# Attention with a gated MLP on one core: opening memsets on two engines, last residual rows in the q/k buffers, another order table

## Chip, core and metric

One core of a Trainium2 chip. The metric is device time in microseconds (us) for one execution of the whole program, taken as the median of three runs. For every kernel there is also one profiled execution, which has a time of its own and a span (first to last instruction) inside it.

## What is computed

Four batches, twelve heads, 448 positions, 64 numbers per head; all in 32-bit floats.

```
scores = (q @ k.T) / sqrt(64), causal mask, softmax with 1e-9 added to the sum
x      = attention output, heads side by side                    # 4 x 448 x 768
h      = gelu_tanh(x @ w_in)                                     # 768 -> 1024
u, v   = halves of h;   v = layernorm(v) * g_ln
v_s    = w_sg @ v + b_sg                                         # mixes positions, 448 x 448
out    = x + (u * v_s) @ w_out                                   # 512 -> 768
```

## The kernel before

The work is cut into 24 pairs of heads (six per batch) and one MLP per batch. A pair (`pair`, L602) loads q and k (L609), makes scores on TensorE in two operations S0 and S1 (L618), adds the mask and takes the row maximum on VectorE (L632, eight operations), takes exponentials with row sums on ScalarE (L640, ten operations, each an ACTIVATE and an accumulator read), turns the weights by TensorE transposes (pairs 0 to 7, L687, evicted to the tile B at L694 or L692) or by a VectorE transpose and block moves by DMA (pairs 8 to 23, L675 and L679), multiplies with v (L718; v is loaded at L712) and scales by the inverse row sums, which take a way through DRAM (L659, L662). The result goes to DRAM as the residual x (L754) and, split into two parts, into the MLP. The MLP (`mlp`) has per batch four groups for v (v0 to v3), four for u, four for the mixing (s) and six for the output (o0 to o5), all as chunks of up to three matmuls at L779. The groups o0 to o5 read back two residual tiles at a time (`res`, L898), add (L910) and store (L914 in the last batch, L918 in the others).

The weight w_in comes in as twelve tiles of 512 KB (W1 to W12, loaded at L552 into three `vn` buffers). Each is prepared by ScalarE (L554), VectorE (L556, L558) and GpSimd (L561, L562). Four tiles of w_sg (SG, L536 to L541) and sixteen of w_out are prepared in a like manner.

Every step is an "op" that is registered with `Order.add`. `Order.plan` sorts the ops of each engine (and of SyncE, which issues all DMAs, in order, each waiting for its semaphores at the head of the queue) by a greedy plan with modelled durations: `dur` of a DMA's issue, `size` for its transfer, and `COLD` = (6.0, 1.35), a factor on transfers issued before 6.0 us. The priorities in that plan are the places in the table `ORDER`, which is written out by hand. Each engine's order in the planned program of the kernel before is the table's own, engine by engine.

What comes first: `consts` (L491, GpSimd: identity and masks), `consts2` (L505, VectorE: zeros into the pad columns of all six P tiles, three fillings of the three `sm` tiles, `mhalf`, the pad rows of `wsg`), `warm` (L521, VectorE: zeros for seven matmuls at L528 that read no data and only keep TensorE busy). VectorE's queue is `consts2`, `warm`, then the masks of pair 0 (two small ones, L556 of W1, a large one).

Score tiles come from six PSUM banks, two for each S op. The fourth S op in the order waits for the exponentials that read the first one's banks, and so on. The tags `qk` (three buffers) and `res` (two buffers) have tiles of the same shape, 128 x 2 x 448.

```
od.add("pool", 2.5, consts, w=["ident", "mask"], at=-9)
od.add("dve", 1.6, consts2, w=["P", "sm", ("wsg", "pad")], at=-9)
od.add("act", 0.2, lambda: nc.scalar.activation(out=pad[:, 0:1], in_=mhalf, func=AF.Exp), ["sm"], ["table"], -30)
od.add("dve", 0.45, warm, w=[wz], at=-30)
rr = buf(two, "res", [128, 2, S])
```

Of the kernel before, what the change touches and what calls it, by code (L numbers as in the profile page):

```python
# [973 lines left out]
```

## Time and profile before

| | before |
|---|---|
| median of 3 runs | 358.58 us (358.38 to 360.68) |
| profiled execution, its own time | 359.28 us |
| its span | 357.5 us, 6919 instructions |
| busy: TensorE / VectorE / ScalarE / GpSimd | 343.3 / 258.7 / 204.2 / 148.9 us |
| chain that ended last | TensorE 55%, ScalarE 15%, issue 11%, VectorE 8%, DMA 5% |

PE is TensorE, PEld its weight loads, DVE VectorE, ACT ScalarE, POOL GpSimd, SP the queue that issues the DMAs. Busy time is time with an instruction in flight; a TensorE operation that stands between two of its own matmuls may count as busy or not. A view of windows gives busy time per engine in a stretch; the chain follows the last instruction back, each time to what released it; a timeline row has the start, the duration and, in brackets, the idle time before it and what ended it. The clock column is the granted TensorE clock as a share of 2.4 GHz.

### The profile page before, as it was taken

To read this page: it belongs to the slowest core of one execution; us is meant where nothing else is said; L and a number is where in the kernel's file an instruction comes from. 1 tells how busy PE (TensorE), PEld (TensorE's weight loads), DVE (VectorE), ACT (ScalarE), POOL (GpSimd) and SP (SyncE) were. 2 spreads that over 40 slices of the span, in tenths; PEclk is the share of its full clock that TensorE was granted. 3 is DMA by queue.
4 is the path that set the end of the run, shared out by engine and by line. 5 is a ranking of instruction groups with operands and counts; after the bars stand their busy time and mean duration, and the time that the engine had idled before them with its cause. 6 is when DMAs were issued, how large, how long until landed. Compare 5 with 4: busy or idle time off the path is not lost.

```text
span 357.5 us, 6919 instructions
## 1 busy us (share of the span) xinstructions
PE 343.3 (96%) x2231; PEld 269.9 (75%) x2231; DVE 258.7 (72%) x801; ACT 204.2 (57%) x658; POOL 148.9 (42%) x185
## 2 busy tenths in 40 slices
PE   5799899999999999999999999999999999999995
PEld 1455566768788887677888887877997797889994
DVE  2877979789999887979889477469679541475512
ACT  2789997975887665682857551544545600344400
POOL 2244777865698820303204821101526510342640
PEclk9969999999999999999999999999999999999999
DMA  7848768989864768987819757985641656700014
GB/s 260 296 126 297 252 202 284 334 283 254 274 173 143 202 157 237 263 272 248 275 22 269 230 149 231 242 284 148 221 119 38 179 146 198 255 5 1 0 53 154
DMA packets 37973, 69.50 MB, mean 194 GB/s; under 512 B 3889, under 2 KB 18993, under 8 KB 37937
## 3 DMA queue, kind: packets, MB, share of 16 engines
q1 hardware_dynamic: 37936, 69.06, 63.5%
q8 instruction: 18, 0.29, 0.3%
q14 instruction: 19, 0.15, 0.1%
HBM read 39.68 MB, written 12.58 MB: 146 GB/s over the span
## 4 chain that ended last, share of the span: by engine, by line
PE 55%; ACT 15%; issue 11%; DVE 8%; DMA 5%; POOL 3%; SPq 2%; DVEq 0%; ACTq 0%; POOLq 0%
PE m L779 41%; ACT P L640 11%; PE s L618 6%; PE o L718 5%; DMA B<-P 5%; DVE P L675 2%; DVE s L632 2%; SPq L679 2%; ACT B L694 2%; PE tx L687 1%; PE ty L687 1%; POOL tmp L884 1%; POOL x L760 1%; PE m L528 1%; ACT vn L554 1%
## 5 line engine op out<-in xcount | busy, mean ns | idle before, releaser
L640 ACT ACTIVATE P<-s,ngm 128x448 f32<-128x448 f32 (+3 forms) x240 | 101.0, 426 | 40.1 <-DVE ngm L632 26.5
L632 DVE CUSTOM_DVE_ANT_0 s<-s,mask 128x192 f32<-128x192 f32 (+3 forms) x192 | 75.2, 444 | 14.6 <-PE s L618 10.5
L779 PE MATMUL m<-win,x 128*128 128x512 f32 (+1 forms) x264 | 66.3, 397 | 0.3 <-ACT P L640 0.3
L779 PE MATMUL m<-x,win 128*128 128x448 f32 x288 | 63.6, 370 | 0.3
L779 PE MATMUL m<-g,wout 128*128 128x448 f32 x288 | 63.1, 369 | 0.4 <-ACT P L640 0.4
L618 PE MATMUL s<-qk 64*66 64x64 f32 (+3 forms) x384 | 55.7, 412 | 2.7 <-ACT P L640 2.3
L779 PEld LDWEIGHTS m<-g,wout 128*128 128x128 f32 x288 | 53.2, 188 | 6.7 <-ACT P L640 1.5
L779 PEld LDWEIGHTS m<-x,win 128*128 128x128 f32 x288 | 53.2, 188 | 6.7 <-ACT P L640 1.1
L779 PEld LDWEIGHTS m<-win,x 128*128 128x128 f32 (+1 forms) x264 | 47.1, 183 | 12.2 <-ACT P L640 0.7
L618 PEld LDWEIGHTS s<-qk 64*128 64x128 f32 (+1 forms) x384 | 33.5, 182 | 25.4 <-issue 13.9
L718 PE MATMUL o<-B,vraw 128*64 128x64 f32 (+4 forms) x672 | 47.8, 293 | 1.3 <-ACT P L640 0.6
L675 DVE STREAM_TRANSPOSE P<-P 128x1024 f32<-128x1024 f32 x32 | 39.2, 1230 | 12.6 <-DMA B<-P 9.3
L640 ACT ACTIVATION_READ_ACCUMULATOR P<-s,ngm 128x1 f32 (+1 forms) x240 | 46.9, 195 | 0.0
L718 PEld LDWEIGHTS o<-B,vraw 128*64 128x64 f32 x672 | 32.8, 137 | 16.0 <-issue 6.6
L779 PE MATMUL m<-wsg,vn 128*128 128x448 f32 x176 | 39.0, 369 | 0.0
L760 POOL TENSOR_TENSOR x<-xt,x 128x448 fp32r<-128x448 f32 x24 | 28.8, 1205 | 22.3 <-ACT x L759 12.6
L779 PEld LDWEIGHTS m<-wsg,vn 128*128 128x128 f32 x176 | 32.7, 188 | 3.2 <-DVE g L792 0.2
L833 POOL TENSOR_TENSOR mv<-mv,mhalf 128x1 f32<-128x1 f32 (+1 forms) x16 | 9.2, 578 | 58.7 <-DVE mv L831 58.6
L884 POOL TENSOR_TENSOR tmp<-tmp,g 128x448 f32<-128x448 f32 x16 | 18.3, 1150 | 20.1 <-DVE tmp L880 20.0
L787 ACT ACTIVATE tmp<-m 128x448 f32<-128x448 f32 (+1 forms) x28 | 15.4, 565 | 18.9 <-PE m L779 17.4
L759 ACT ACTIVATE x<-xt 128x448 fp32r<-128x448 f32 x18 | 10.2, 574 | 27.9 <-DVE xt L748 27.8
L632 DVE DVE_READ_ACCUMULATOR2_ANT ngm<- 128x1 f32 (+1 forms) x192 | 25.7, 134 | 0.0
(72 smaller groups left out, 382.7 us busy)
## 6 DMA issues: line engine op xcount, KB each, us to landing
B<-P SPq DMA_DIRECT2D x64, 256.0 KB
qk<-in_qk_dram SPq DMA_DIRECT2D x24, 448.0 KB
vn<-in_w_in_dram SPq DMA_DIRECT2D x12, 512.0 KB
vraw<-in_vP_dram SPq DMA_DIRECT2D x24, 256.0 KB
rb<-rd SPq DMA_DIRECT2D x24, 256.0 KB
xd<-xt SPq DMA_DIRECT2D x24, 224.0 KB
res<-xd SPq DMA_DIRECT2D x12, 448.0 KB
out_dram<-res SPq DMA_DIRECT2D x9, 448.0 KB
```

The lines of the kernel that those rows point to most:

```text
L618: nc.tensor.matmul(out=s[z][bk].t[0:w, col:col + n], lhsT=qk_.t[r, 0, q0:q0 + w], rhs=qk_.t[r, 1, 0:n], start=True, stop=True)
L632: nc.vector.tensor_tensor_reduce(out=o, in0=o, in1=mk, scale=-0.125, scalar=3e38, op0=ALU.add, op1=ALU.min, accum_out=ngm[ib[z]][c][0:m])
L640: act(n, lambda c=c, m=m, r0=r0, k0=k0, n=n, bk=bk, col=col, off=off, kc=kc, i=i, z=z: nc.scalar.activation(out=P[i][r0:m, off:off + n], i ...
L675: dve(PW, lambda z=z: nc.vector.transpose(A[ia][:, :, :, z, :].rearrange("p g t k -> p t g k"), P[ib[z]]), Pk[z] + ["P"], Ak, Tt, 1.105)
L679: dma(lambda i=i: nc.sync.dma_start(out=B_.t[:, 512 * i:512 * i + 512], in_=PP[ia][32 * i:32 * i + 32].rearrange("p (g n) -> p g n", g=4)) ...
L718: nc.tensor.matmul(out=dst(o.t[r]), lhsT=vr.t[:, c, r], rhs=src(z), start=first and n == 0, stop=last and n == len(lst) - 1)
L759: act(S, lambda: nc.scalar.activation(out=y.t[:, 0:S], in_=x.t, func=AF.Copy), [x], [y], Ty, True)
L760: pool_tt(S, lambda: nc.gpsimd.tensor_tensor(out=y.t[:, S + 64:], in0=x.t, in1=f(y.t)[:, 0:S], op=ALU.subtract), [x, y], [(y, 1)], Ty)
L779: nc.tensor.matmul(out=ps.t[0:l().shape[1], 0:n], lhsT=l(), rhs=rr(), start=(k == 0), stop=(k == len(mms) - 1))
L787: act(n, lambda: nc.scalar.activation(out=z(), in_=h(), func=AF.Square), [ps], [t], at)
L833: od.add("pool", 0.46, lambda mv=mv, m=m: nc.gpsimd.tensor_tensor(out=mv.t[0:m, 1:2], in0=mv.t[0:m, 1:2], in1=mhalf[0:m], op=ALU.pow), ["s ...
L884: pool_tt(S, lambda z=z, u=u: nc.gpsimd.tensor_tensor(out=z(), in0=z(), in1=u.t, op=ALU.mult), [u], [t], at)
```

## The change

1. The opening memsets are split. `consts2` on VectorE keeps the pads of P tiles 0 and 1, the filling of `sm` tile 0, and `mhalf`. A new op `consts3` on GpSimd, behind `consts`, does P tiles 2 to 5, `sm` tiles 1 and 2 and the pad rows of `wsg`. What reads P tiles 0 and 1 or `sm` tile 0 first waits for VectorE's op, the rest for GpSimd's.
2. In the last batch the residual tiles `res` are taken from the three `qk` buffers.
3. Modelled prices are set anew: `COLD` 6.0, 0.85; issue times 0.43 to 1.7 for five kinds of DMA; the size of the load of `g_ln` and `b_sg` is halved. They act only through the plan.
4. The table `ORDER` is a new one, of 1927 ops (the new op is number 2). `WHEN`, `ctx`, `seq` and `key` are bookkeeping; with `WHEN = 0, 0` the ops are registered in the old order. `xt` keeps its two buffers.

```
-SLOTS = {'qk': 3, 'B': 2, 'rb': 3, 'vraw': 2}
+SLOTS = {'qk': 3, 'B': 2, 'rb': 3, 'vraw': 2, 'xt': 2}
+WHEN = 0, 0
-COLD = 6.0, 1.35
+COLD = 6.0, 0.85
...
+    def pads(eng, ps, sms):
+        for i in ps:
+            for c in (320, 960):
+                eng.memset(P[i][:, c:c + 64], 0.0)
+        for t in sms:
+            eng.memset(t, 0.0)
+            eng.memset(t[:, :, :, 2:3], 1e-9)
+            eng.memset(t[64:128, :, 0, 0:1], 1.0)
+
     def consts2():
...
+        pads(nc.vector, (0, 1), sm[:1])
         nc.vector.memset(mhalf, -0.5)
-        nc.vector.memset(f(wsg)[64:128, 3, 1, :], 0.0)
...
+    def consts3():
+        pads(nc.gpsimd, range(2, NP), sm[1:])
+        nc.gpsimd.memset(f(wsg)[64:128, 3, 1, :], 0.0)
+
+    od.add("dve", 0.75, consts2, w=["P0", "sm0"], at=-9)
+    od.add("pool", 2.4, consts3, w=["P", "sm", ("wsg", "pad")], at=-8)
...
-        dma(load, [], [t], at - 6, n * 512, early)
+        dma(load, [], [t], at - 6, n * 512, early, dur=0.43 * len(src))
...
+        kp, ks = "P" if p % (NP // 2) else "P0", "sm" if p % NS else "sm0"
...
-                rr = buf(two, "res", [128, 2, S])
+                rr = buf(*((two, "res") if b < B - 1 else (some[SLOTS["qk"]], "qk")), [128, 2, S])
```

What the two tables say of the first ops, engine by engine (S0, S1 scores; Tx, Ty transposes; ex3, ex0, ex2, ex1, ex1b exponentials by chunk; z0 and z1 the heads of a pair; ev an eviction; V the load of v):

```
SyncE   before  qk0 W1 V0 qk1 qk2 W2 W3 gb V1 qk3 W4 qk4 ...
SyncE   after   qk0 W1 qk1 qk2 W2 W3 gb V0 V1 qk3 W4 qk4 W5 SG1 SG2 SG3 ...
VectorE before  consts2 warm, masks of pair 0: 0z1 0z0, W1/L556, 3z0 1z0 1z1 2z0, W1/L558, 2z1 3z1, masks of pair 1
VectorE after   consts2 warm, W1/L556 W1/L558, masks of pair 0: 0z0 0z1 3z0 3z1 1z0 1z1 2z0 2z1, W2/L556, masks of pair 1
ScalarE before  W1, pair 0: ex3z0 ex0z0 ex2z0 ex1z0 ex1bz0 ex1z1 ex2z1 ex3z1 ex1bz1 ex0z1, pair 1: ex3z0 ...
ScalarE after   W1, pair 0: ex3z0 ex3z1 ex0z0 ex0z1, W2, ex2z0 ex1z1, W3, ex1bz0 ex2z1, p1 ex3z1, ex1z0, p1 ex0z1 ex3z0, ex1bz1, p1 ...
TensorE before  p0S0 p0S1 p1S0 p1S1 p0Tx p0Ty p2S0 p0Tx ... p4Tx behind 1 chunk of the first MLP, p5Ty behind 2
TensorE after   p0S0 p0S1 p1S0 p1S1 p0Ty p2S0 p0Tx p0Ty ... p3Tx behind 3 chunks of the first MLP, p4Tx behind 4, p5Ty behind 6
GpSimd  after   consts consts3 W1/L561 W1/L562 W2 ...
```

In the last batch, SyncE's table now has the residual load of o0 and o1 in front of the block moves of pair 22, the one of o2 and o3 between the moves of pairs 22 and 23, and the one of o4 and o5 ahead of the first store; before, the first two stood behind all moves and the third behind two stores. TensorE's last chunks before: o3 o3 o4 o5 o5 o5 o5 o4 o3 o2 o2 o3 o4 o4; after: o1 o2 o2 o3 o5 o5 o5 o5 o4 o4 o4.

## Rows read from the trace of the kernel before

**Rows 1.** Busy time by windows; columns: stretch, length, busy (instructions), clock, DMA share, GB/s

```profile
0.00:4.00 4.00, 0.00 (x0) 0.00 (x0) 2.40 (x24) 1.49 (x2) 2.63 (x11) 1.00 0.53 167
4.00:7.20 3.20, 3.08 (x7) 0.88 (x7) 0.07 (x1) 0.66 (x1) 0.00 (x0) 1.00 0.95 289
7.20:10.00 2.80, 2.80 (x13) 1.68 (x14) 0.50 (x5) 0.00 (x0) 0.00 (x0) 1.00 1.03 417
...
16.00:24.00 8.00, 7.50 (x29) 4.49 (x29) 4.70 (x20) 7.15 (x25) 2.31 (x2) 0.57 0.40 138
24.00:30.00 6.00, 5.87 (x47) 3.37 (x47) 4.99 (x22) 5.57 (x23) 1.96 (x2) 1.00 0.86 249
30.00:54.00 24.00, 22.16 (x164) 13.76 (x163) 19.95 (x69) 23.46 (x79) 17.25 (x18) 1.00 0.77 254
54.00:120.00 66.00, 65.77 (x455) 50.27 (x454) 61.32 (x199) 50.27 (x159) 50.22 (x71) 1.00 0.78 243
```

**Rows 2.** The chain that ended last, in order of time, 0 to 60 us

```profile
0.82 0.93 DVE P L508 x12
3.00 0.43 DVE wsg L514
3.58 0.50 DVE tmp L523
4.12 3.17 PE m L528 x7
7.29 2.06 PE s L618 x8
...
9.97 0.28 DVE vn L556
...
10.95 0.73 ACT P L640 x2
...
54.49 0.66 PE ty L687 x4
55.25 1.39 PE m L779 x6
```

**Rows 3.** Timeline of the first 16 us, all engines

```profile
0.73 0.21 POOL masks.py:197 MEMSET ident<- 128x128 f32 x1 [0.29 <-POOLq L963]
...
1.25 0.47 POOL L493 MEMSET mask<- 128x448 bf16 x1
...
2.97 0.45 POOL L500 TENSOR_SCALAR_AFFINE_SELECT mask<-mask 64x320 bf16<-64x320 bf16 x1
...
6.48 0.66 ACT L554 ACTIVATE vn<-vn 128x512 f32<-128x512 f32 x1 [3.40 <-DMA vn<-in_w_in_dram]
...
9.50 0.23 DVE L632 CUSTOM_DVE_ANT_0 s<-s,mask 64x64 f32<-64x64 f32 x1 [5.44 <-PE s L618]
...
11.79 0.68 DVE L558 SCALAR_TENSOR_TENSOR vn<-vn 128x512 int32<-128x512 int32 x1
...
12.60 0.64 POOL L561 CAST win<-vn 128x512 fp32r<-128x512 f32 x1 [9.18 <-DMA vraw<-in_vP_dram]
```

**Rows 4.** Timeline of ScalarE, 18 to 26 us

```profile
20.57 0.60 ACT L694 ACTIVATE B<-tx 128x512 f32<-128x512 f32 x1 [0.56 <-PE tx L687]
...
24.28 0.60 ACT L694 ACTIVATE B<-tx 128x512 f32<-128x512 f32 x1 [0.53 <-PE tx L687]
```

**Rows 5.** Timelines of the end, in small windows

```profile
338.93 14.76 PE L779 MATMUL m<-g,wout 128*128 128x448 f32 x72
...
348.74 0.38 SPq L898 DMA_DIRECT2D res<-xd  x1
...
353.72 0.62 DVE L910 TENSOR_TENSOR res<-m,res 128x448 f32<-128x448 f32 x1
354.05 0.93 SPq L914 DMA_DIRECT2D out_dram<-res  x2
```

**Rows 6.** The chain again, 157 to 164 us: a block move

```profile
157.91 5.63 DMA B<-P
```

More of the change, by code (lines that the diff above doesn't have):

```diff
@@ L223, in __init__ @@
         self.shared, self.room, self.early = shared, room, early
-        self.bufs = {}
+        self.bufs, self.ctx, self.seq = {}, (), {}
     def add(self, eng, dur, fn, r=(), w=(), at=0.0, done=0.0, rows=1.0, size=0.0, early=0.0, shape=None, port=False,
@@ L228, in add @@
         n = len(self.ops)
+        self.seq[self.ctx] = k = self.seq.get(self.ctx, -1) + 1
+        key = self.ctx + (k,)
         deps = set()
@@ L503, in attention_gated_mlp @@
     od.add("pool", 2.5, consts, w=["ident", "mask"], at=-9)
-    def consts2():
-        for i in range(NP):
-            for c in (320, 960):
-                nc.vector.memset(P[i][:, c:c + 64], 0.0)
-        for t in sm:
-            nc.vector.memset(t, 0.0)
-            nc.vector.memset(t[:, :, :, 2:3], 1e-9)
-            nc.vector.memset(t[64:128, :, 0, 0:1], 1.0)
-        nc.vector.memset(mhalf, -0.5)
-        nc.vector.memset(f(wsg)[64:128, 3, 1, :], 0.0)
-    od.add("dve", 1.6, consts2, w=["P", "sm", ("wsg", "pad")], at=-9)
-    od.add("act", 0.2, lambda: nc.scalar.activation(out=pad[:, 0:1], in_=mhalf, func=AF.Exp), ["sm"], ["table"], -30)
+    def pads(eng, ps, sms):
[6 more added lines that the diff above has]
+            eng.memset(t[64:128, :, 0, 0:1], 1.0)
+    def consts2():
+        pads(nc.vector, (0, 1), sm[:1])
+        nc.vector.memset(mhalf, -0.5)
+    def consts3():
[3 more added lines that the diff above has]
+    od.add("pool", 2.4, consts3, w=["P", "sm", ("wsg", "pad")], at=-8)
+    od.add("act", 0.2, lambda: nc.scalar.activation(out=pad[:, 0:1], in_=mhalf, func=AF.Exp), ["sm0"], ["table"], -30)
     def warm():
@@ L533, in split_w @@
     def split_w(src, dst, key, n, at, rows=128, early=0.0):
+        od.ctx = key
         t = buf(three, "tmp", [128, 512])
@@ L546, in split_w64 @@
     def split_w64(src, dst, key, n, at, pool_, tag, words, early=0.0):
+        od.ctx = key
         t = buf(pool_, tag, *words)
@@ L574, in weights_b @@
     def weights_b():
+        od.ctx = ("gb",)
         def load():
@@ L577, in load @@
             nc.sync.dma_start(out=bB, in_=bass.AP(tensor=b_sg.tensor, offset=b_sg.offset, ap=[[0, 128], [1, S]]))
-        dma(load, [], ["gb"], 20, 459e3, LATER["g"])
+        dma(load, [], ["gb"], 20, 231e3, LATER["g"], dur=1.7)
         def halve():
@@ L585, in weights_b, with weights_s @@
         dve(512, halve, ["gb"], ["gb"], DUE["gb"])
+    def weights_s():
         t0 = start(HP) + MLP[0] + DUE["wo"]
@@ L591, in weights_b, with weights_o @@
                 ("wsg", 3), S, t0 + 23, 64, LATER["s"])
-        for c in range(FC):
+    def weights_o(cs):
+        t0 = start(HP) + MLP[0] + DUE["wo"]
+        for c in cs:
             for a in range(0, DM, WO):
@@ L602, in pair @@
         b, hp = divmod(p, HP)
+        od.ctx = ("pair", p)
         T = start(p) + PAIR[p]
@@ L642, in pair @@
                     bias=ngm[i][c][r0:m], scale=-1.0, accum_out=sm[ip][r0:m, z, kc[0], kc[1]:kc[1] + 1]),
-                    [s[z][bk], ("ngm", i, c), "P", "sm"] + ([("P", i, k - 1)] if k == 1 else [("P", i, 2)] if k == 4 else []),
+                    [s[z][bk], ("ngm", i, c), kp, ks] + ([("P", i, k - 1)] if k == 1 else [("P", i, 2)] if k == 4 else []),
                     [("P", i, k), ("sm", ip, z, k)], T + due("ex", b), extra=2)
@@ L651, in inv @@
             nc.vector.reciprocal(out=rs, in_=tot)
-        od.add("dve", 0.323, inv, sk + ["sm"], ["rs"], T + due("inv", b))
+        od.add("dve", 0.323, inv, sk + [ks], ["rs"], T + due("inv", b))
         rb, sb = buf(some[SLOTS["rb"]], "rb", [128, 512]), s[1][1]
@@ L660, in copies @@
                                   in_=rT[ip][4 * z:4 * z + 4].unsqueeze(1).broadcast_to([4, 16, 128]))
-        dma(copies, [("rT", ip)], [("rd", ip)], T + due("r", b), 65e3)
+        dma(copies, [("rT", ip)], [("rd", ip)], T + due("r", b), 65e3, dur=0.64)
         dma(lambda: nc.sync.dma_start(out=rb.t, in_=bass.AP(
             tensor=rd[ip].tensor, offset=rd[ip].offset, ap=[[512, 32], [0, 4], [1, 512]])), [("rd", ip)], [rb],
-            T + due("r", b), 262e3)
+            T + due("r", b), 262e3, dur=0.56)
         Tt = T + per + due("T", b)
@@ L675, in pair @@
                 dve(PW, lambda z=z: nc.vector.transpose(A[ia][:, :, :, z, :].rearrange("p g t k -> p t g k"), P[ib[z]]),
-                    Pk[z] + ["P"], Ak, Tt, 1.105)
+                    Pk[z] + [kp], Ak, Tt, 1.105)
             for i in (0, 2, 1, 3):
@@ L700, in pair @@
                     (u(tx)[:, 0::7, :], 896), (tx.t[:, 64:192], 384), (tx.t[:, 192:320], 0), (tx.t[:, 320:448], 512)]),
-                   Pk[z] + ["ident", "P"], [tx], Tt)
+                   Pk[z] + ["ident", kp], [tx], Tt)
                 evict(z, 0, tx)
@@ L704, in pair @@
                     (u(ty)[:, 0:4:3, :], 256), (ty.t[:, 64:192], 768), (ty.t[:, 256:384], 128), (ty.t[:, 384:512], 640)]),
-                   Pk[z] + ["ident", "P"], [ty], Tt)
+                   Pk[z] + ["ident", kp], [ty], Tt)
                 evict(z, 1, ty)
@@ L710, in pair @@
         Ty = T + per + due("xs", b)
-        vr, o, x = buf(some[SLOTS["vraw"]], "vraw", [128, 4, 2 * D]), bank("o"), buf(two, "xt", [128, S])
+        vr, o, x = buf(some[SLOTS["vraw"]], "vraw", [128, 4, 2 * D]), bank("o"), buf(some[SLOTS["xt"]], "xt", [128, S])
         dma(lambda: nc.sync.dma_start(out=vr.t, in_=vP[b, hp]), [], [vr], T + due("V", b), 262e3, T + due("V", b) - 4)
@@ L807, in mlp @@
             ps = bank("m")
+            od.ctx = ("v", b, tcn)
             at = step(3.89 if m == 128 else 2.6)
@@ L833, in mlp @@
             od.add("pool", 0.46, lambda mv=mv, m=m: nc.gpsimd.tensor_tensor(
-                out=mv.t[0:m, 1:2], in0=mv.t[0:m, 1:2], in1=mhalf[0:m], op=ALU.pow), ["sm"], [mv], at)
+                out=mv.t[0:m, 1:2], in0=mv.t[0:m, 1:2], in1=mhalf[0:m], op=ALU.pow), ["sm0"], [mv], at)
             dve(DH, lambda mv=mv, z=z, m=m: nc.vector.tensor_scalar(
@@ L848, in mlp @@
             vn[tcn] = y
+        if b == 0:
+            for k in range(2):
+                if WHEN[k] == 1:
+                    (weights_s, lambda: weights_o(range(FC)))[k]()
         for dc in range(FC):
             ps = bank("m")
+            od.ctx = ("u", b, dc)
             at = step(3.4) + due("mu", b)
@@ L861, in mlp @@
             gelu2(ps, 128, S, at + 3.4 + due("post", b), uT[dc])
+        if b == 0:
+            for k in range(2):
+                if WHEN[k] == 2:
+                    (weights_s, lambda: weights_o(range(FC)))[k]()
         for dc in range(FC):
             ps = bank("m")
+            od.ctx = ("s", b, dc)
             at = step(2.08) + due("ms", b)
@@ L891, in mlp @@
             ps = bank("m")
+            od.ctx = ("o", b, mc)
             at = step(2.27) + due("mo", b)
@@ L926, in attention_gated_mlp @@
             weights_b()
+            for k in range(2):
+                if WHEN[k] == 0:
+                    (weights_s, lambda: weights_o(range(FC)))[k]()
         mlp(b)
```

2 lines of the change are left out of this document (1 added, 1 removed), and 192 rows, old and new, of the table ORDER.

## The prediction

> **What bounds the kernel now.** I read the windows first, since a share over the whole span mixes stages. From 54 us on TensorE is busy 65.77 of 66 us [rows 1], and it stays so to the end: what is left to gain lies ahead of 54 us and in the last few us. From 30 to 54 us ScalarE is the full engine, 23.46 of 24.00 us, with TensorE at 22.16 [rows 1]. The chain says the same in order of time [rows 2]: VectorE's memsets (0.82 to 4.08), seven warm-up matmuls (to 7.29), the scores of pair 0, masks, then ScalarE from its first exponential at 10.95 to shortly before 54.49, where TensorE takes over. So three stretches follow one another: a start of 10.95 us before ScalarE has its real work; some 43 us of ScalarE; then TensorE alone. An edit pays if it brings the first exponential forward, or closes gaps of ScalarE ahead of 54 us; a gap closed later on ScalarE, VectorE or the DMA queues pays nothing.
>
> The start itself is a row of waits. The warm-up waits for VectorE's last memset [rows 2], and pair 0's scores begin at 7.29 with no wait other than the warm-up's end, though q and k were the first load to be issued: by 7.20 the DMA engines had moved 167 x 4 + 289 x 3.2 = 1,590 KB [rows 1], and that load is the first 459 KB of them. VectorE then sat 5.44 us until 9.50 [rows 3].
>
> **The change, part by part.**
>
> *Memsets.* VectorE loses 8 of 12 pad memsets, which took 0.93 together: 0.62. The three fillings and `mhalf` are ten memsets between 1.75 and 3.00, 0.125 each; six go: 0.75. The `wsg` rows (start 3.00) and the step to the next memset (3.58) go: 0.58 [rows 2]. Sum 1.95: the warm-up runs from 2.17 to 5.34 and pair 0's scores start at 5.34. That is no gain of 1.95 yet, for something else is late next: VectorE's queue now has both steps of W1 ahead of all masks. W1 was there at 6.48; L554 takes 0.66 [rows 3], L558 0.68 behind it, a handover about 0.1: VectorE is free at 7.9. The scores are ready by 5.34 + (9.50 - 7.29) = 7.55. So W1 decides, and the first mask stands at 7.95 instead of 9.50. Before, 1.45 lay between it and the first exponential, with L556 in between (0.28 on the chain, [rows 2]); that is gone from there: 1.17. First exponential: 9.12 instead of 10.95. **Gain 1.83** (bounds: 1.45 if the handovers cost more, 2.2 if W1 is earlier).
>
> *The same memsets on GpSimd.* Fifteen more, behind `consts`, which ends at 2.97 + 0.45 = 3.42 [rows 3]. No row shows a 64-column memset there. One of 128 columns took 0.21, one of 448 two-byte columns 0.47 [rows 3]; so 14 small ones cost 0.10 to 0.21 each and the `wsg` rows 0.47 to 0.95: 1.9 to 3.9, end between 5.3 and 7.3. I take 2.6, from the 128-column row with part of its columns. GpSimd's next work is the cast of W1, which waits for L558 at 7.9; before, it stood at 12.60 after 9.18 us of idle time [rows 3]. Cost nothing. The wait that it adds sits in ScalarE's queue: pair 1's first exponential needs this op, at about 13 us, with all exponentials behind it. Without this cover each us past 13 would be a us of the kernel.
>
> *The new places of W2 and W3.* ScalarE now prepares W2 and W3 between pair 0's exponentials, so it waits there if they have not landed. Ahead of W2's end stand q0, W1, q1, q2, W2: 448 + 512 + 448 + 448 + 512 KB, 2.42 MB. Up to 10.0 us the engines moved 0.67 + 0.92 + 1.17 = 2.76 MB [rows 1]: W2 is there at about 9.2, W3 (0.52 MB more) at about 10.5. ScalarE wants them near 10.9 and 12.4. No wait. V of pair 0 moves behind them and the g/b load, past seven issues of SyncE; its user is the first weighted sum, 10 us later and more. Cost nothing.
>
> *The order in ScalarE's stretch.* I counted the two tables. Up to pair 5's last exponential ScalarE has 60 exponentials, 14 evictions and 4 w_sg tiles in both; w_in tiles 8 before, 10 after: +1.2 us at about 0.6 each, with L554's 0.66 as the top end. TensorE has, ahead of the transposes of pair 5, six chunks of the first MLP instead of two; two chunks took 1.39 [rows 2], so four are +2.8. ScalarE does more earlier and TensorE wastes less while it waits. What counts is where TensorE last waits for ScalarE. Before, its worst stand is at the transposes of pairs 3 to 5; after, pair 3's transposes need the same exponentials behind one more w_in tile, and have three chunks in front. The two about cancel there, so I book 0 (bounds: -0.6, the tile; +1.4, two chunks that fall into time lost so far).
>
> *ScalarE's gaps.* From 16 to 24 it sat 8.00 - 7.15 = 0.85, from 24 to 30 0.43 [rows 1], the largest two for a transpose to evict, 0.56 and 0.53 [rows 4], while TensorE ran at 0.57 of its clock. The new order gives TensorE a start 1.95 earlier but pair 0's heads end later, since W2, W3 and two exponentials of pair 1 stand between them. I take half of the 1.28: **0.6** (bounds -1.1 to 1.28).
>
> *The end.* The third residual load waited until 348.74 for a buffer that a store had to leave [rows 5]; the qk buffers are idle by then, so that wait goes. But TensorE runs 14.76 us without a gap from 338.93, to 353.69, and the last add starts at 353.72 in either order: the loads decide nothing. What moves is SyncE: its last two issues took 0.93 from 354.05, so the last began near 354.52, 0.18 after the add's end at 354.34. The new order ends o2, o3 and o5 earlier, and SyncE is free: **0.15** (0 to 0.4).
>
> Sum: 1.83 + 0 + 0.6 + 0.15 = 2.58. The profiled execution took 359.28 with a span of 357.5, 0.70 above the median of 358.58; its counterpart would be 356.7, and the median **356.0**.
>
> **Rivals.**
>
> *A: TensorE's clock takes part of it back (357.7).* Between pair 1's scores and pair 0's first transposes TensorE now has nothing: head 0's last exponential is ScalarE's twelfth, not its fifth, so it ends about 5.8 us after 9.12 instead of some 2.4 after 10.95. Before, TensorE's idle time around 14 to 16 us was followed by a window at 0.57, that is mostly at 1.2 GHz [rows 1]. If the longer hole brings as much again, ScalarE's two waits for evictions [rows 4] double instead of halving: 0.6 and 1.1 are lost, leaving 0.9. For it: the hole. Against it: warm-up and scores run unbroken from 2.17, earlier than before. The Trainium skill, TensorE: Matmul & The Clock Gate, "What's actually happening", has the clock at half after idle time and at full after sustained work, by a window that does not start with the kernel. By that rule this rival would come true in some executions and not in others; the 0.57 row agrees with its first half, the second no run here shows.
>
> *B: ScalarE's stretch closes up (354.8).* All of 1.28 and the 0.54 it sat between 30 and 54 us [rows 1] go: 1.83 + 1.28 + 0.54 + 0.15 = 3.80. If two chunks count as well, 353.4. For it: loads of W4 to W7 start sooner, since W1's buffer is free after a cast at 8 instead of 12.60. Against: gaps of this kind come from handovers between engines, which stay.
>
> *C: slower (362).* SyncE issues in order. The new table sets two residual loads of the last batch among the block moves of pairs 22 and 23; each waits at the queue's head for stores of x to land and for a qk buffer, and the moves wait behind it. A block move took 5.63 us on the chain [rows 6]. If a move comes late by one such length and TensorE has no other chunk ready, 356.0 + 5.6 = 361.6. It decides from the point where the hold exceeds the matmuls of the last MLPs that are ready. Against it: the stores were issued well ahead, and the buffers' last readers, the scores of pairs 21 and 22, stand long before.
>
> *D: nothing comes of it (358.4).* GpSimd's memsets end after 13 us, so pair 1 waits and the start's gain is gone. That needs four times the 2.6.
>
> **How the numbers follow.** Forecast 0.50, its own range 354.9 to 357.2; A 0.17; B 0.22; C 0.07; D 0.04. A change of 1% is 3.6 us, about what a measurement of this kernel tells from none: faster means below 355.0, slower above 362.2. Faster takes B and an eighth of the forecast: 0.29. Slower takes the upper half of C and a little for what the table moves elsewhere: 0.06. The rest, 0.65, lies within. The range takes in B with its chunks at the low end and A and D with half a us of spread at the high end: 353.4 to 359.4.
>
> **What would show it.** Right: warm-up at 2.2 us, first exponential near 9.1, ScalarE without a gap until about 19, TensorE's last wait for ScalarE before 54 us, the last add ending 2.5 us earlier. Wrong: a first mask that waits for scores; ScalarE waiting for DMA at W2 or W3; a clock row below 0.57 or for longer; any TensorE gap of over 1 us behind 60 us.

## The result, and the profile after

| | before | after |
|---|---|---|
| median | 359.03 us (356.81 to 360.68, 12 runs) | 355.83 us (354.45 to 358.71, 12 runs) |
| ratio | | 0.9915, 95% interval 0.9888 to 0.9942 |
| profiled execution: own time, span | 359.28, 357.5 us | 355.13, 353.3 us |
| busy: TensorE / VectorE / ScalarE / GpSimd | 343.3 / 258.7 / 204.2 / 148.9 us | 340.8 / 257.3 / 203.9 / 150.3 us |

The change saves 3.1 to 3.2 us, 0.85%: the interval does not reach 1, and the saving lies within the 1% that was set as "the same". Forecast were 356.0 us and 2.6 saved. The two profiled executions lie 4.15 us apart, more than the medians; where single executions scatter is read from the runs below. Executions more than 1.5% above the fastest of their kernel (one each in E2, E5 and E8, two in E10) count in the medians but not in the ratios.

In the changed kernel the line numbers are higher: the pad memsets stand at L512 to L516, the `wsg` rows at L524, the warm-up at L533 and L538, the w_in steps at L566 to L574, the scores at L639, masks L653, exponentials L661, transposes L708, evictions L715, MLP matmuls L800, the last adds L943.

The timeline of the first 10 us of the changed kernel, against [rows 3] and the head of [rows 2]:

```profile
0.81 0.33 DVE L512 MEMSET P<- 128x64 f32 x4 [0.81 <-PEq L999]
...
2.12 3.17 PE L538 MATMUL m<-tmp 128*128 128x512 bf16 x7 [2.12 <-DVE tmp L533]
...
3.47 0.75 POOL L512 MEMSET P<- 128x64 f32 x8
...
5.03 0.47 POOL L524 MEMSET wsg<- 64x448 f32 x1
...
7.12 0.69 DVE L570 SCALAR_TENSOR_TENSOR vn<-vn 128x512 int32<-128x512 int32 x1 [0.30 <-ACT vn L566]
7.73 0.22 DVE L653 CUSTOM_DVE_ANT_0 s<-s,mask 64x64 f32<-64x64 f32 x1
...
7.94 0.64 POOL L573 CAST win<-vn 128x512 fp32r<-128x512 f32 x1 [2.44 <-DVE vn L570]
...
8.87 0.64 ACT L661 ACTIVATE P<-s,ngm 128x448 f32<-128x448 f32 x1 [1.78 <-DVE ngm L653]
```

VectorE is through with its memsets at about 2.1 instead of 4.1, and the warm-up starts there. The first mask has no bracket: it waits for nothing but the w_in step ahead of it in VectorE's queue. GpSimd's share runs from 3.47 to 5.50, 2.03 us, and 2.44 us of idle time follow before the first cast. The first exponential moves from 10.95 to 8.87.

The windows of the changed kernel, against [rows 1] (stretch, length, busy time and instructions of PE, PEld, DVE, ACT, POOL, then the granted clock, DMA share, GB/s):

```profile
16.00:24.00 8.00, 8.00 (x41) 5.63 (x40) 6.56 (x26) 7.90 (x30) 4.11 (x4) 0.69 0.82 263
24.00:30.00 6.00, 5.23 (x44) 3.21 (x41) 4.73 (x20) 5.85 (x20) 4.27 (x4) 1.00 0.76 230
30.00:54.00 24.00, 23.44 (x177) 15.65 (x176) 21.28 (x77) 22.99 (x82) 18.54 (x21) 1.00 0.91 298
...
75.00:353.30 278.30, 272.50 (x1781) 224.95 (x1779) 198.53 (x558) 140.49 (x442) 104.04 (x128) 1.00 0.60 174
```

ScalarE sat idle for 0.10 us from 16 to 24 and 0.15 from 24 to 30; before it was 0.85 and 0.43 [rows 1]. From 30 to 54 the picture turns over: ScalarE now has 1.0 us of idle time there and TensorE only 0.6; before, it was 0.5 and 1.8. The chain of the changed kernel shows when that happens:

```profile
8.87 1.92 ACT P L661 x8
10.79 0.56 ACT vn L566
...
37.09 0.50 ACT B L715
...
37.63 0.96 PE m L800 x3
```

The chain runs through ScalarE from the first exponential to 37.6 us and through TensorE from there; before, TensorE took over at 54.49 [rows 2]. The second line is the second w_in tile, taken up with no wait for its load.

The last windows row is the ruler for all that follows. From 75 us on the clock is 1.00, so TensorE's busy time there is the work that it still has to do, and length minus busy time is what it wastes from there to the end. The same stretch of the kernel before:

```profile
75.00:357.50 282.50, 277.24 (x1802) 229.05 (x1798) 202.87 (x573) 143.04 (x449) 106.70 (x132) 1.00 0.60 177
```

At 75 us the changed kernel has 277.24 - 272.50 = 4.74 us less to do. Behind 75 us it wastes 278.30 - 272.50 = 5.80 us, the kernel before 5.26. So 4.74 won, 0.54 given back: 4.20, the difference of the spans. (Every profile here has the same 2231 TensorE records, 2228 with four warm-up matmuls, so the measure does not hang on missing records. But busy time is not work alone: six kernels below that are nearly the same ahead of 75 us have 1780 to 1782 records left there and still differ by 1.3 us, and smaller differences are not read.)

What TensorE waited for from 75 to 345 us, in the kernel before:

```profile
PE m L779 <- ACT P L640: 0.7, 2, 0.4
PE o L718 <- DVE rT L655: 0.5, 1, 0.5
```

and in the changed kernel (columns: us in total, times, longest):

```profile
PE m L800 <- ACT P L661: 1.0, 1, 1.0
PE s L675 <- DVE rs L672: 0.8, 1, 0.8
PE m L800 <- ACT B L715: 0.2, 1, 0.2
```

These are other places: a chunk of batch 2's first MLP at 221.8 us and the transpose of pair 10's reciprocals at 116.9 us. The end, against [rows 5], from timelines of the last 10 us:

```profile
342.75 7.06 PE L800 MATMUL m<-g,wout 128*128 128x448 f32 x34
...
349.84 0.62 DVE L943 TENSOR_TENSOR qk<-m,qk 128x448 f32<-128x448 f32 x1 [1.14 <-PE m L800]
...
350.49 0.33 SPq L947 DMA_DIRECT2D out_dram<-qk  x1
```

From the last matmul's end (349.81) to the end of the span are 3.5 us; before, 353.69 to 357.5, 3.8. This tail is the larger part of what is wasted behind 75 us: without it the changed kernel wastes 2.3 us there and the kernel before 1.5.

### The profile page after: what moved, and what is told of

It reads as the page before. It is cut to its first block, busy times and chain, and to the rows that moved or that the text cites. A ratio compares the mean times of both kernels' runs of the same rounds, so it can differ in the third digit from the quotient of the medians.

```text
span 353.3 us, 6901 instructions
## 1 busy us (share of the span) xinstructions
PE 340.8 (96%) x2231; PEld 270.5 (77%) x2231; DVE 257.3 (73%) x786; ACT 203.9 (58%) x658; POOL 150.3 (43%) x200
## 4 chain that ended last, share of the span: by engine, by line
PE 63%; ACT 13%; DVE 11%; DMA 8%; issue 2%; SPq 2%; POOL 0%; DVEq 0%; ACTq 0%
PE m L800 43%; PE o L739 9%; ACT P L661 8%; PE s L639 8%; DMA B<-P 4%; DVE s L653 2%; DVE P L696 2%; DMA vn<-in_w_in_dram 1%; ACT B L715 1%; DMA rd<-rT 1%; DMA g<-in_w_out_dram 1%; DVE g L570 1%; PE tx L708 1%; ACT vn L566 1%; SPq L700 1%
## 5 line engine op out<-in xcount | busy, mean ns | idle before, releaser
L661 ACT ACTIVATE P<-s,ngm 64x64 f32<-64x64 f32 (+3 forms) x240 | 100.9, 426 | 44.5 <-DVE P L696 25.4
L653 DVE CUSTOM_DVE_ANT_0 s<-s,mask 128x192 f32<-128x192 f32 (+3 forms) x192 | 75.4, 444 | 1.6 <-PE s L639 1.5
L800 PE MATMUL m<-win,x 128*128 128x512 f32 (+1 forms) x264 | 66.6, 398 | 1.3 <-ACT P L661 1.0
L800 PE MATMUL m<-g,wout 128*128 128x448 f32 x288 | 63.0, 369 | 0.0
L800 PE MATMUL m<-x,win 128*128 128x448 f32 x288 | 62.6, 367 | 0.2 <-ACT B L715 0.2
L800 PEld LDWEIGHTS m<-g,wout 128*128 128x128 f32 x288 | 53.3, 188 | 6.2 <-issue 0.9
L800 PEld LDWEIGHTS m<-x,win 128*128 128x128 f32 x288 | 53.8, 188 | 5.4 <-ACT B L715 0.6
L800 PEld LDWEIGHTS m<-win,x 128*128 128x128 f32 (+1 forms) x264 | 47.0, 183 | 13.4 <-ACT P L661 1.3
L639 PE MATMUL s<-qk 64*66 64x64 f32 (+3 forms) x384 | 54.8, 412 | 0.3 <-ACT P L661 0.3
L781 POOL TENSOR_TENSOR x<-xt,x 128x448 fp32r<-128x448 f32 x24 | 27.9, 1167 | 54.6 <-ACT x L780 35.8
L639 PEld LDWEIGHTS s<-qk 64*128 64x128 f32 (+1 forms) x384 | 33.5, 181 | 21.0 <-issue 13.9
L739 PE MATMUL o<-B,vraw 128*64 128x64 f32 (+4 forms) x672 | 47.0, 292 | 0.1
L661 ACT ACTIVATION_READ_ACCUMULATOR P<-s,ngm 128x1 f32 (+1 forms) x240 | 47.0, 196 | 0.0
L800 PE MATMUL m<-wsg,vn 128*128 128x448 f32 x176 | 41.0, 372 | 0.2
L800 PEld LDWEIGHTS m<-wsg,vn 128*128 128x128 f32 x176 | 32.3, 188 | 4.7 <-POOL vn L863 1.0
L811 ACT ACTIVATE tmp<-tmp 128x448 f32<-128x448 f32 (+2 forms) x32 | 19.0, 603 | 12.8 <-DVE tmp L809 12.7
L653 DVE DVE_READ_ACCUMULATOR2_ANT ngm<- 128x1 f32 (+1 forms) x192 | 25.7, 134 | 0.0
```

The costliest lines, as they stand in the source:

```text
L639: nc.tensor.matmul(out=s[z][bk].t[0:w, col:col + n], lhsT=qk_.t[r, 0, q0:q0 + w], rhs=qk_.t[r, 1, 0:n], start=True, stop=True)
L653: nc.vector.tensor_tensor_reduce(out=o, in0=o, in1=mk, scale=-0.125, scalar=3e38, op0=ALU.add, op1=ALU.min, accum_out=ngm[ib[z]][c][0:m])
L661: act(n, lambda c=c, m=m, r0=r0, k0=k0, n=n, bk=bk, col=col, off=off, kc=kc, i=i, z=z: nc.scalar.activation(out=P[i][r0:m, off:off + n], i ...
L739: nc.tensor.matmul(out=dst(o.t[r]), lhsT=vr.t[:, c, r], rhs=src(z), start=first and n == 0, stop=last and n == len(lst) - 1)
L781: pool_tt(S, lambda: nc.gpsimd.tensor_tensor(out=y.t[:, S + 64:], in0=x.t, in1=f(y.t)[:, 0:S], op=ALU.subtract), [x, y], [(y, 1)], Ty)
L800: nc.tensor.matmul(out=ps.t[0:l().shape[1], 0:n], lhsT=l(), rhs=rr(), start=(k == 0), stop=(k == len(mms) - 1))
```

## The experiments

The first four take the change apart. E1 to E4 ran beside the same kernel before (358.63 us), E5 to E8 beside it at 358.66, E9 and E10 at 358.76. The order of every engine was written out in these kernels in place of the plan, so that an edit moves only what it names.

**E1: the split memsets alone.** Every engine's order is that of the kernel before, the residual tiles have their own two buffers again.

```diff
 def run(self):
-    for n in self.plan():
+    for n in ORDER:
...
-rr = buf(*((two, "res") if b < B - 1 else (some[SLOTS["qk"]], "qk")), [128, 2, S])
+rr = buf(two, "res", [128, 2, S])
```

> The kernel before, each engine in its old order, with the memsets split and nothing else. Theory 1 (the start and the table pay separately): warm-up at 2.1 us, first exponential about 9.0 instead of 10.95, and since ScalarE bounds the stretch up to 54 us most of it arrives: 1.5 to 2.0 us below the kernel before. Rival (the old order cannot use an early start, because its transposes wait for evictions while TensorE is at its lower clock, and W2 and W3 stand behind V): first exponential at 9.0 all the same, but ScalarE's gaps up to 30 us grow by 1 us or more, and 0 to 0.7 us arrive.

Measured: 355.6 us, ratio 0.9928 (0.9901 to 0.9954). Its first exponential and its windows:

```profile
8.38 0.64 ACT L661 ACTIVATE P<-s,ngm 128x448 f32<-128x448 f32 x1 [1.18 <-DVE ngm L653]
```

```profile
16.00:24.00 8.00, 8.00 (x50) 4.86 (x52) 6.99 (x26) 7.91 (x30) 4.04 (x4) 0.79 0.51 137
24.00:30.00 6.00, 5.24 (x34) 3.04 (x31) 5.21 (x22) 5.88 (x22) 2.33 (x3) 1.00 0.95 303
...
75.00:353.89 278.89, 273.56 (x1771) 226.44 (x1769) 199.06 (x554) 140.68 (x439) 103.51 (x128) 1.00 0.60 176
```

In the old order the first two small masks stand ahead of the w_in steps, so the first exponential comes at 8.38, 2.57 earlier than before. Of TensorE's work 277.24 - 273.56 = 3.7 us less is left at 75 us: more than the 2.57, because ScalarE's idle time from 16 to 30 us went as well, from 0.85 + 0.43 [rows 1] to 0.09 + 0.12, in an execution whose clock from 16 to 24 us was 0.79 where the kernel before had 0.57 [rows 1]. The saving was larger than the 1.5 to 2.0 expected: by the medians the split alone brings 3.0 us, as much as the whole change.

**E2: the new table alone.** All memsets on VectorE; order and residual tiles as changed.

```diff
-pads(nc.vector, (0, 1), sm[:1])
+pads(nc.vector, range(NP), sm)
 nc.vector.memset(mhalf, -0.5)
+nc.vector.memset(f(wsg)[64:128, 3, 1, :], 0.0)
...
-pads(nc.gpsimd, range(2, NP), sm[1:])
-nc.gpsimd.memset(f(wsg)[64:128, 3, 1, :], 0.0)
```

> The changed kernel with all opening memsets back on VectorE. Theory 1: warm-up at 4.1, scores of pair 0 at 7.3, first mask about 9.5 and first exponential about 10.6; the 1.75 us go through to the end: 1.5 to 2 us above the changed kernel, so the table alone is worth 1.2 to 2 us against the kernel before. Rival (the start was a by-product, the new order hides it because W1 to W3 decide when ScalarE gets on): at most 0.7 us above the changed kernel.

Measured: 357.11 us, ratio 0.9957 (0.9934 to 0.998).

```profile
10.59 0.63 ACT L661 ACTIVATE P<-s,ngm 128x448 f32<-128x448 f32 x1 [3.47 <-DVE ngm L653]
```

```profile
16.00:24.00 8.00, 8.00 (x27) 4.63 (x26) 6.09 (x26) 7.88 (x34) 3.41 (x5) 0.51 0.67 197
24.00:30.00 6.00, 6.00 (x41) 3.86 (x39) 4.82 (x21) 5.54 (x18) 4.20 (x5) 0.80 0.77 232
...
75.00:356.69 281.69, 275.77 (x1795) 227.56 (x1794) 200.00 (x564) 142.20 (x447) 104.91 (x128) 1.00 0.60 175
```

The table saves 1.5 us by the median and 277.24 - 275.77 = 1.5 us by the work left. So at 75 us the two parts nearly add up: 3.7 + 1.5 = 5.2 against 4.7 together. By the medians they do not: 3.0 + 1.5 against 3.1. Above the changed kernel are 1.3 us by the medians, between theory 1 and the rival, and 3.3 by the work left, for a first exponential that comes 1.7 later. The lower clock, 0.51 and 0.80 here against 0.69 and 1.00 there, may have the rest; the runs do not part the two.

**E3: the residual tiles back.** The changed kernel with `res` in its own two buffers and the three residual loads of the last batch at their old places.

```diff
-rr = buf(*((two, "res") if b < B - 1 else (some[SLOTS["qk"]], "qk")), [128, 2, S])
+rr = buf(two, "res", [128, 2, S])
```

> The changed kernel with the last batch's residual tiles in their own two buffers again, and so with their loads at the old places, behind the stores that free them. Theory 1 (loads decide nothing, TensorE's last matmul does): within 0.4 us of the changed kernel, third load about 345 to 349 us, end 3.5 to 3.8 us behind the last matmul. Rival (the early loads are what lets the last adds and stores run dry): 1 us or more slower.

Measured: 356.24 us, ratio 0.9947 (0.9917 to 0.9977). The end of this kernel, by timeline:

```profile
342.75 6.45 PE L800 MATMUL m<-g,wout 128*128 128x448 f32 x31
...
345.80 0.38 SPq L931 DMA_DIRECT2D res<-xd  x1
...
349.72 1.22 DVE L943 TENSOR_TENSOR res<-m,res 128x224 f32<-128x224 f32 x3 [4.12 <-DMA res<-xd]
```

TensorE is through at 349.20, 0.61 earlier than in the changed kernel, and yet the span is 353.9: VectorE sat idle for 4.12 us until the third residual load, issued at 345.80, had landed, and from the last matmul to the end it is 4.7 us instead of 3.5. Under the new order, in which o2, o3 and o5 end earlier, the residual rows in the qk buffers are worth 1.2 us at the end: the tail is 3.5 us in all eight profiles that have them under this order. Theory 1 has the load's time right and the end wrong. The medians lie only 0.4 us apart, which these runs cannot tell from none. Under the old order there is no such wait: E1 keeps the old buffers too and its last five adds wait for TensorE.

**E4: six MLP chunks late.** The changed kernel with the six chunks of batch 0's first MLP that TensorE's table had moved ahead of the transposes of pairs 3 to 5 back where they were.

```diff
 TensorE's queue, from the order table
-... p3Tx behind 3 chunks of the first MLP, p4Tx behind 4, p5Ty behind 6 ...
+... p4Tx behind 1 chunk of the first MLP, p5Ty behind 2, the other four behind pair 5's first step ...
```

> The changed kernel with the first six chunks of the first MLP on TensorE moved back to the places they had before: one ahead of pair 4's turned sums, one behind its third transposes, four behind pair 5's. Theory 1 (the chunks fill time that TensorE loses to ScalarE): TensorE loses as much as they fill, 1 to 2.5 us slower than the changed kernel, and TensorE waits for ScalarE up to 45 us or later instead of 37. Rival (ScalarE's earlier start and order are all of it): within 0.4 us.

Measured: 358.22 us, ratio 0.9989 (0.9966 to 1.0012): 2.4 us slower than the changed kernel. Its chain, where TensorE takes over, and its work left:

```profile
51.20 0.56 DVE B L713
...
51.89 0.63 PE ty L708 x4
```

```profile
75.00:358.15 283.15, 275.64 (x1795) 227.56 (x1794) 200.18 (x564) 141.94 (x447) 104.87 (x128) 1.00 0.61 174
```

With the first exponential at 8.82, as in the changed kernel, the chain stays with ScalarE and VectorE until 51.9 us again, and 275.64 - 272.50 = 3.1 us more is left at 75 us. So the chunks fill time that TensorE would lose while ScalarE is behind; they are what lets it take over at 37.6. This one piece is larger than what the whole table saves alone (1.5), so other parts of the table cost something. How much, E1 shows beside E4: the changed kernel without this piece (358.22) is 2.6 us slower than the split with the old order (355.6). With the split in place the pieces of the new order cancel in the times.

**E5: the first masks ahead of the w_in steps.** E1 pointed to it: its first exponential is half a us earlier than the changed kernel's.

```diff
 VectorE's queue, from the order table
-consts2 warm W1/L568 W1/L570 0z0 0z1 3z0 3z1 1z0 ...
+consts2 warm 0z0 0z1 3z0 3z1 W1/L568 W1/L570 1z0 ...
```

> The changed kernel with one edit: the first four masks of pair 0 (two 64x64, two 128x448) stand ahead of the two VectorE steps of the first w_in tile (L568, L570) instead of behind them. Theory 1 (the first exponential sets the beat of ScalarE's stretch, and the w_in steps now stand in its way): the first mask goes from 7.73 us to about 6.9, the first exponential from 8.87 to 8.2 to 8.5, and the time falls by 0.3 to 0.6 us, to about 355.4. Theory 2 (TensorE, which takes over from ScalarE at 37 us, has cover enough by then, and GpSimd's two steps of the tile come 1.5 us later): the first exponential moves as said and the time does not, within 0.3 us.

Measured: 355.91 us, ratio 0.9904 (0.9866 to 0.9941), against 355.83. The first exponential came at 8.60 (8.2 to 8.5 was expected), and the chain has

```profile
37.66 0.97 PE m L800 x3
```

The handover stands where it stood, at 37.66 instead of 37.63. Theory 2: a quarter of a us at the start of ScalarE's stretch is not felt at its end.

**E6: fewer warm-ups.** The changed kernel with a start that is over 1 us shorter.

```diff
 TensorE's, VectorE's and ScalarE's queues, from the order table
-warm x7, p0S0 ...
+warm x4, p0S0 ...
-consts2 warm W1/L568 W1/L570 0z0 0z1 3z0 3z1 1z0 1z1 2z0 2z1 ...
+consts2 warm 0z0 0z1 3z0 3z1 1z0 1z1 2z0 2z1 W1/L568 W1/L570 ...
-W1, ex3z0 ex3z1 ex0z0 ex0z1, W2, ex2z0 ex1z1, W3, ex1bz0 ex2z1 ...
+W1, ex3z0 ex3z1 ex0z0 ex0z1 ex2z0 ex1z1, W2, ex1bz0 ex2z1, W3 ...
```

> The changed kernel with 4 warm-up matmuls instead of 7, all eight masks of pair 0 ahead of the first w_in tile's VectorE steps, and the squares of the second and third w_in tile two exponentials later on ScalarE. Theory 1 (start-up time before the first exponential is paid one for one): the scores of pair 0 begin near 4.0 us instead of 5.2, the first exponential comes near 7.3 instead of 8.87, and the time falls by 1.0 to 1.5 us, to about 354.5. Theory 2 (the clock takes it back): the granted clock of 16 to 24 us is lower or the low stretch lasts longer, and the time stays within 0.5 us of the changed kernel. Theory 3 (what waits for the w_in tiles takes it back): the first chunks of the MLP come later than in the changed kernel and TensorE waits for GpSimd's product, and the time rises.

Measured: 356.75 us, ratio 0.994 (0.9914 to 0.9966): not faster than the changed kernel. Scores began at 3.93 and the first exponential at 7.68, 1.2 us earlier. Then:

```profile
8.52 2.06 PE L639 MATMUL s<-qk 64*128 64x448 f32 x16 [1.65 <-DMA qk<-in_qk_dram]
...
10.93 0.68 ACT L566 ACTIVATE vn<-vn 128x512 f32<-128x512 f32 x1 [0.49 <-DMA vn<-in_w_in_dram]
```

```profile
16.00:24.00 8.00, 6.10 (x24) 4.15 (x26) 7.19 (x28) 7.55 (x26) 4.21 (x4) 0.71 0.79 258
24.00:30.00 6.00, 6.00 (x42) 3.16 (x40) 2.81 (x11) 4.85 (x18) 4.06 (x4) 0.81 0.90 300
```

```profile
19.41 2.07 PE s L639 x5
...
38.67 0.96 PE m L800 x3
```

The earlier start ran into two loads: pair 1's scores waited 1.65 us for their q and k and ended at 10.58, later than in the changed kernel (10.09), and ScalarE waited 0.49 us for the second w_in tile. ScalarE, which the changed kernel keeps busy for 5.85 of the 6 us from 24 to 30, has work for 4.85 here: from 19.4 us the chain runs through TensorE at 0.71 and 0.81 of its clock (below 1.00 it is for part of the stretch at 1.2 GHz instead of 2.4), and the handover comes 1.0 us later than before, not earlier. From 16 to 24 us TensorE also stood idle for 1.90 us, which it does not in the changed kernel. Of theory 2 the longer low stretch is there (0.81 where the changed kernel has 1.00), but the time is 0.9 above the changed kernel's, outside its 0.5. Of theory 3 the later chunk and the longer time are there, but no wait for GpSimd's product is among TensorE's waits up to 75 us. How much the clock, the loads and the moved steps each took is not settled.

**E7: the split alone, with fewer warm-ups.** E1 with the old order.

```diff
 TensorE's and VectorE's queues, from the order table
-warm x7, p0S0 ...
+warm x4, p0S0 ...
-consts2 warm 0z1 0z0 W1/L568 3z0 ...
+consts2 warm 0z1 0z0 3z0 W1/L568 ...
```

> The kernel with the old order table and the split memsets alone, with 4 warm-up matmuls instead of 7, and the first VectorE step of the first w_in tile behind the first large mask. Theory 1 (start-up paid one for one): the first exponential comes near 7.2 us instead of 8.38, and the time falls by 0.8 to 1.2 us against the split alone (355.6), to about 354.6. Theory 2 (the scores wait for the q and k transfer, which lands when it lands, or the clock takes it back): the first exponential moves by less than 0.5 us, or it moves and the time stays within 0.4 us of the split alone.

Measured: 355.3 us, ratio 0.9884 (0.9852 to 0.9916), against 355.6 for E1: no difference that the runs can tell.

```profile
3.97 3.63 PE L639 MATMUL s<-qk 64*128 64x448 f32 x16
8.40 2.06 PE L639 MATMUL s<-qk 64*128 64x448 f32 x16 [0.80 <-DMA qk<-in_qk_dram]
```

```profile
7.54 0.63 ACT L661 ACTIVATE P<-s,ngm 128x448 f32<-128x448 f32 x1 [0.31 <-DVE ngm L653]
```

```profile
16.00:24.00 8.00, 8.00 (x47) 5.06 (x47) 6.66 (x25) 6.67 (x25) 4.28 (x4) 0.70 0.52 155
```

The first exponential came 0.84 us earlier than in E1, and from 16 to 24 us ScalarE worked 6.67 us against 7.91 there, at a clock of 0.70 against 0.79: 1.24 us lost for 0.84 won, in the profiled executions. This one was the longest of the seven (358.73 us; the others 353.61 to 356.69), so the median does not rest on this loss. It also shows that TensorE hardly gained: pair 0's scores began 1.24 us earlier than in E1 but took 3.63 us instead of 2.44 and ended at 7.60 instead of 7.65, and pair 1's waited for their q and k until 8.40 (8.56 in E1). Both parts of theory 2 are seen, the transfer and the clock; what each costs is not settled.

**E8: GpSimd's memsets three times.**

```diff
 def consts3():
-    pads(nc.gpsimd, range(2, NP), sm[1:])
+    for _ in range(3):
+        pads(nc.gpsimd, range(2, NP), sm[1:])
```

> The changed kernel with GpSimd's share of the pad memsets (eight of 128x64, and the small ones) done three times over, so that GpSimd's start-up work grows from 2.0 us to about 5.2 and ends near 8.6 us instead of 5.5. Theory 1 (the memsets on GpSimd are covered until the first w_in tile needs GpSimd at 7.94): about 0.7 us of GpSimd's delay reaches the first w_in tile's cast, none of it the first exponential, and the time rises by no more than 0.5 us. Theory 2 (something of the first pairs waits for those buffers, or GpSimd and VectorE share their way to the memory): VectorE's first masks or ScalarE's exponentials come later or take longer, and the time rises by 1 us or more.

Measured: 354.98 us, ratio 0.9881 (0.985 to 0.9912), as low a median as any here, with more work. (Line numbers are one higher here.)

```profile
8.54 0.47 POOL L525 MEMSET wsg<- 64x448 f32 x1
9.07 0.71 POOL L574 CAST win<-vn 128x512 fp32r<-128x512 f32 x1
...
9.09 0.64 ACT L662 ACTIVATE P<-s,ngm 128x448 f32<-128x448 f32 x1 [1.79 <-DVE ngm L654]
```

GpSimd's share ends at 9.01 instead of 5.50 and holds the first cast up by 1.1 us, to 9.07; the first exponential is at 9.09 and the handover at 37.84, both 0.2 later than in the changed kernel. So 3.5 us more on GpSimd cost nothing that can be measured: the cover is real, and it is wide. Why the median is low is not shown; it is one of six runs.

**E9: the two late waits.** Read across the profiles, waits at these two of TensorE's steps, at 117 and 222 us, are in every profile of the new order (the changed kernel, E2 to E6, E8) and in none of the old order (before, E1, E7). E9 moves TensorE's two waiting steps behind what follows them.

```diff
 TensorE's queue, from the order table (Tr: transpose of a pair's reciprocals; b2v1.0: first chunk of a group of batch 2's first MLP)
-... p10Tr p9PV0 p9PV1 p9PV2 ...
+... p9PV0 p9PV1 p10Tr p9PV2 ...
-... b2v1.0 b1o5.3 b2v0.2 b2v1.1 ...
+... b1o5.3 b2v0.2 b2v1.0 b2v1.1 ...
```

> The changed kernel with two of TensorE's steps moved in its order table, because in every profile of the new order TensorE waits at these two places and in no profile of the old order: the transpose of pair 10's reciprocals (L675, 0.8 us at 117 us, for VectorE) goes behind two steps of pair 9's product with V, and the first chunk of a first-MLP group of batch 2 (L800, 1.0 us at 222 us in the changed kernel, up to 1.4 in others, for ScalarE) goes behind the two chunks that follow it. Theory 1 (the new order gives back behind 75 us, at these places, a part of what it gains before): both waits go from the profile, TensorE's idle time behind 75 us falls from 5.8 us to about 4, and the time falls by 1.5 to 2 us, to about 354. Theory 2 (the waits only move on to the next instruction that hangs on the same transfers): the idle time behind 75 us stays within 0.5 us of 5.8 and the time within 0.5 us of the changed kernel.

Measured: 354.97 us (353.32 to 357.31, 12 runs), ratio 0.991 (0.988 to 0.9941). TensorE's waits from 75 to 345 us, all of them, and the window:

```profile
PE m L800 <- ACT B L715: 0.2, 1, 0.2
```

```profile
75.00:351.54 276.54, 272.60 (x1781) 225.24 (x1779) 198.35 (x559) 140.51 (x443) 103.96 (x128) 1.00 0.60 176
```

Both waits are gone and nothing has taken their place: 276.54 - 272.60 = 3.94 us wasted behind 75 us, as theory 1 had it (about 4), against 5.80. The work left is that of the changed kernel, 272.60 against 272.50. The span fell by 1.8 us. The medians show less, 0.9, and the means less still: that of the 12 runs lies 0.6 us below that of the changed kernel's 22 (12 in the result, 10 in E10); drawn again 20,000 times from the same runs, 95 in 100 of such differences lie between 1.4 and -0.2. It is faster than the kernel before; that it is faster than the changed kernel too is shown for the profiled execution and not by the times.

**E10: the changed kernel again.**

```diff
 def run(self):
-    for n in self.plan():
+    for n in ORDER:
```

> The changed kernel as it is, with its order written out instead of planned, as a second profile and a second set of times beside the run above. If TensorE's work in the first 75 us is fixed by the order and only its idle time behind them varies from execution to execution, the work left at 75 us is within 1 us of the changed kernel's 272.5 us, the two waits at 117 and 222 us are there again, and the time is 355.8 within 0.6. If the first 75 us vary as much as the rest, the work left differs by more than 1 us.

Measured: 355.86 us (352.73 to 358.83, 12 runs), ratio 0.9919 (0.9884 to 0.9953).

```profile
16.00:24.00 8.00, 7.54 (x44) 5.07 (x40) 6.70 (x27) 7.90 (x30) 4.12 (x4) 0.79 0.89 296
...
75.00:353.14 278.14, 272.17 (x1780) 225.30 (x1779) 198.62 (x558) 140.70 (x443) 103.65 (x128) 1.00 0.61 175
```

```profile
PE m L800 <- ACT B L715: 0.8, 1, 0.8
PE s L675 <- DVE rs L672: 0.8, 1, 0.8
PE m L800 <- ACT P L661: 0.6, 1, 0.6
...
```

The work left agrees within 0.4 us, and the two waits are there again, the one for VectorE at the same length, the other at 0.6 instead of 1.0, with a third beside them.

The work left at 75 us and the waste behind it, from the windows row of each profile as above:

| | work left | waste behind 75 us | own time | median |
|---|---|---|---|---|
| before | 277.24 | 5.26 | 359.28 | 358.6 to 359.0 |
| E2 table alone | 275.77 | 5.92 | 358.47 | 357.11 |
| E4 chunks late | 275.64 | 7.51 | 359.96 | 358.22 |
| E7 split, warm 4 | 275.16 | 6.84 | 358.73 | 355.3 |
| E1 split alone | 273.56 | 5.33 | 355.67 | 355.6 |
| E6 warm 4 | 273.52 | 5.98 | 356.27 | 356.75 |
| E5 masks first | 272.86 | 7.84 | 357.54 | 355.91 |
| after | 272.50 | 5.80 | 355.13 | 355.83 |
| E10 after, again | 272.17 | 5.97 | 354.91 | 355.86 |
| E3 residuals back | 271.83 | 7.12 | 355.72 | 356.24 |
| E9 two waits | 272.60 | 3.94 | 353.32 | 354.97 |
| E8 pads thrice | 271.60 | 5.40 | 353.82 | 354.98 |

In E3, E5, the changed kernel, E8, E9 and E10, which differ little ahead of 75 us, TensorE takes over at 37.5 to 38.0 us and has 271.6 to 272.9 us left. The waste behind 75 us is what scatters: 5.40 to 7.84 with the same late order (E3's 7.12 has the longer tail in it). E5's profiled execution is 2.4 us longer than the changed kernel's, and 2.04 of it is waste.

## Why the prediction was right, point by point

The forecast of 356.0 us stands beside 355.83, within its own narrow range, and the verdict "within 1%" was the likeliest. The sum of its terms is less good than its total, and that the total comes so near is luck: some terms were too small, and what they lacked was lost to costs that were not in the sum.

- **The memsets: right.** Warm-up at 2.12 (forecast 2.17). "So W1 decides": the first mask stands directly behind the w_in step, at 7.73 (7.95), with no wait for scores. First exponential 8.87 (9.12): a gain of 2.08 where 1.83 was booked, inside its bounds of 1.45 to 2.2. In time the split alone brought 3.0 us (E1); in its profile ScalarE's gaps closed with it.
- **The memsets on GpSimd: right.** 2.03 us against 2.6 (1.9 to 3.9), end at 5.50 within 5.3 to 7.3. "Cost nothing" held with 3.5 us more on GpSimd (E8). Rival D is out.
- **W2 and W3: right.** ScalarE takes W2 up at 10.79 behind an exponential that ends there, with no wait for the load. (V of pair 0 moves past six issues, not seven; nothing hangs on it.)
- **ScalarE's gaps: undersized.** Half of 1.28 was booked, 0.6; 1.28 - 0.25 = 1.03 went. In this step rival B was nearer; its 354.8 or 353.4 us in all did not come. The gaps were booked as the new order's doing, but in E1 they closed in the old order too, at a clock of 0.79. What the new order adds is that they stay closed: ScalarE works 7.88 to 7.90 of the 8 us from 16 to 24 in the changed kernel, E3, E4, E5, E8, E9 and E10, at clocks from 0.61 to 0.83, while in the old order it works 7.15 at 0.57 (before) and 6.67 at 0.70 (E7).
- **The order in ScalarE's stretch: the 0 came out, its working failed.** Beside the split the whole table saves nothing in the times (355.6 for E1, 355.83) and 1.1 us by the work left. It was booked at 0, with +1.4 as the upper end, "two chunks that fall into time lost so far". The working looked for TensorE's worst stand at the transposes of pair 3, and set an extra w_in tile against three chunks there. What the runs show: put back, the six chunks cost 2.4 us (E4), and with them TensorE takes over at 37.6 and not shortly before 54. The sign "TensorE's last wait for ScalarE before 54" was fulfilled by 16 us more than meant. The rest of the table costs about as much, 2.6 us from E1 to E4; which parts, beside the two late waits, was not tried one by one.
- **The end: right by luck.** 0.15 was booked (0 to 0.4), 0.3 measured. But "the loads decide nothing" fails for the new order: without the qk buffers VectorE waits 4.12 us for the third load, and the end takes 1.2 us longer (E3). That is by profiles; the medians of E3 and the changed kernel do not part. The statement was worked out from the old order's tail, in which TensorE's last stretch covers the load.
- **What was not in the sum: the new order's late waits.** "A TensorE gap of over 1 us behind 60 us" was named as a sign of error. The listed ones are 1.0 and 0.8, just under it. Removed, they give 1.8 us in the profile (E9). By the medians the change would have saved 0.9 us more without them, which is not clear of the scatter.
- **Rival A, the clock: not in the changed kernel.** Its granted clock from 16 to 24 us was 0.69 and not below 0.57 [rows 1]; ScalarE's waits for evictions went. Its sign, a clock row below 0.57 or for longer, came with the table alone: 0.51 and then 0.80 (E2). In E6 and E7 it may have a share in taking back 0.8 to 1.2 us of earlier start, beside the loads.
- **Rival C, the order of SyncE: not seen.** No wait of TensorE at the end; the last stretch runs to 349.81 without a gap.

So the total came out by errors of opposite sign: +0.25 at the first exponential, +0.4 in the gaps, up to +2.4 for the chunks, +0.15 at the end, against the costs of the rest of the table, 2.6 us from E1 to E4, of which 1.8 us in two late waits are seen in one profile and the remainder is not found.
